# Frequency sets mirrored in PSUM, half-piece sums by accumulating DMAs and the fourth up-product last in a fixed order

## Chip, cores and metric

One core of a Trainium2 chip runs the program. TensorE (PE) multiplies, ScalarE (ACT) empties PSUM and computes activations, VectorE (DVE) does elementwise work in SBUF, GpSimd (POOL) does a few small operations and issues the DMAs of its queue, and SyncE (SP) issues the other DMAs. The metric is the device time of one execution in microseconds (us), as the median of several runs.

## What is computed

Two branches of one input x = A_q (2048 rows, 640 columns, bf16) are mixed row by row:

```python
g = sigmoid((x * gate_w).sum(-1, keepdims=True))
# branch A: long convolution by FFT over 2048 rows (padded to 4096), one per column
kv = shift_conv(k, shift_k, 4 taps) * v
y = irfft(rfft(kv, 4096) * rfft(ssm_k, 4096))[:2048]
a = x * (y + kv * ssm_D)
# branch B: a mixer and an MLP
h = gelu(layernorm(x) @ w1)            # 640 -> 640
x1 = x + shift_groups(h) @ w2
b = x1 + gelu(layernorm(x1) @ w3) @ w4 # 640 -> 1536 -> 640
out = g * a + (1 - g) * b
```

## The kernel before

Rows are kept as 2 chunks (c) of 128 partitions by 8 (rho). Branch B goes over four groups sc of two rho: mm1 (L967), mm2 (L1075), the third product ("up-product", L1129, 240 matmuls of 512 columns), then the fourth ("down-product", L1147, 4 x 24 matmuls of 320 columns for each sc). Each down-product is seeded by ACT, which copies x1 to PSUM (L1057), and is emptied by ACT with the factor 1 - g.

Branch A works on two column halves of 320. For each half and each of the signals h (the filter) and k (the convolved input):

- `forward` (L1167) multiplies by cosine and sine tables on PE (L1178). Frequencies are in two sets, kap 0 and kap 1; set 1 mirrors set 0. In set 0 each of 4 residues r and 2 parts (real, imaginary) takes 4 matmuls. In set 1 the even r add 2 matmuls to what set 0 left in PSUM (table FM2), the odd r take 4 of their own (FM1). ACT empties each result (128x640) into a slot, tags Sh and Sk.
- `unit` (L1277) is DVE's part, one per half and set: a butterfly on the h slot, a window (two adds) and a butterfly on the k slot, the complex product, and the fold. Slots hold 16 rows of 320 elements; sums and differences run mostly on whole slots, 128x2560 and 128x1280. One sum of each product, 128x2560, is made by a DMA that adds into its target (`add_dma`, L700, issued by POOL).
- `inverse` (L1313) multiplies by the inverse tables on PE: 8 output residues rho of 8 matmuls for each half (L1366, and L1341 for the last four of the second half, column chunk by chunk). ACT scales by g into one of four buffers XN (tag gy), DVE multiplies by q (`fin`), the sum with branch B goes into X by an accumulating DMA (first half, L1392) or by DVE (second half), and SP stores the rows.

All instructions are nodes of a graph. `schedule` and `_forward` (L181, L200) pick the next node of all engines by a modelled start time, with the list RANK as the priority among equals, and also pick the PSUM bank pair (4 pairs) of each job. Each engine then runs its nodes in that order and waits on semaphores for the rest. Every DVE add, subtract or multiply is recorded at L663, every eviction at L694, the second layernorm's ACT operations at L680, the DVE halves at L1351 to L1356. In the order that results, the last things on PE are the last four inverse rows of the second half. They can be multiplied only after DVE has finished the second half's last unit.

Of the kernel before, what the change touches and what calls it, by code (L numbers as in the profile page):

```python
# [7 lines left out]
U16 = mybir.dt.uint16  # L8
# [4 lines left out]
PAIRS = 4  # L13
# [75 lines left out]
class Prog:  # L89
    LAT = {"pe": (0.0, 0.20), "act": (0.24, 0.16), "dve": (0.12, 0.12), "pool": (0.2, 0.2), "sp": (0.1, 0.1)}  # L90
    LOOK = 1.0

# [86 lines left out]
    PRIO = ()  # L179

    def schedule(self):  # L181
        for n in self.nodes:
            n.base = frozenset(n.deps)
        for j in self.jobs:
            own = set(j.nodes)
            j.ext = [d for v in j.nodes if not v.first for d in v.base if d not in own]
            if j.seeded:
                j.nodes[0].soft = [d for v in j.pes for d in v.base if d not in own]
        for n in self.nodes:
            for d in n.deps:  # L190
                d.users.append(n)
        for n in self.nodes:
            n.prio = self.PRIO[n.idx]
        self._forward()

    RATE = 390e3
    WINDOW = 3.4133
    PHASE = 2.4

    def _forward(self):  # L200
        nodes = self.nodes
        for n in nodes:
            n.deps = set(n.base)
            n.missing = len(n.deps)
            n.start = n.end = None
        for j in self.jobs:
            j.pair = None
            j.left = len(j.evicts) if j.evicts else 1
        free = {"pe": 1.0, "act": 0.7, "dve": 0.8, "pool": 1.1, "sp": 0.7}
        ready = {e: [] for e in ENGS}  # L210
        known_at = {}
        pair_free = [0.0] * PAIRS
        pair_job = [None] * PAIRS
        bits = [[False, False] for _ in range(PAIRS)]
        link = 0.0
        xlink = 0.0
        alink = 0.0
        slink = 0.0
        warm = False
        window = -1  # L220
        duty = carry = 0.0
        busy, lock = False, 0.0
        LAT = self.LAT

        def arrive(n):
            at = 0.0
            for d in n.deps:
                t = d.end + (LAT[d.eng][0 if d.eng == n.eng else 1] if d.kind == "c" else 0.05)
                if t > at:
                    at = t  # L230
            known_at[n] = at
            ready[n.eng].append(n)

        for n in nodes:
            if n.missing == 0:
                arrive(n)
        left = len(nodes)
        order = {e: [] for e in ENGS}
        allseq = []
        while left:  # L240
            best = None
            for e in ENGS:
                for n in ready[e]:
                    t = max(known_at[n], free[e])
                    if n.first:
                        j = n.job
                        tp = None
                        for i in range(PAIRS):
                            if pair_job[i] is not None and pair_job[i].left:
                                continue  # L250
                            if j.seeded and not (bits[i][0] and bits[i][1]):
                                continue
                            if tp is None or pair_free[i] < tp:
                                tp = pair_free[i]
                        if tp is None:
                            continue
                        t = max(t, tp)
                        ok = True
                        for d in j.ext:
                            if d.end is None:  # L260
                                ok = False
                                break
                            if not n.seed:
                                t = max(t, d.end - n.cost)
                        if ok and n.seed:
                            for d in n.soft:
                                if d.end is None:
                                    ok = False
                                    break
                                t = max(t, d.end - self.LOOK)  # L270
                        if not ok:
                            continue
                    key = (t, -n.prio, n.idx)
                    if best is None or key < best[0]:
                        best = (key, n)
            assert best is not None, "schedule is stuck"
            n = best[1]
            e = n.eng
            t = best[0][0]
            ready[e].remove(n)  # L280
            n.start = t
            cost = n.cost
            if n.array:
                w = int((t - self.PHASE) // self.WINDOW)
                while window < w:
                    warm = duty > (0.42 if warm else 0.75) * self.WINDOW
                    window += 1
                    duty, carry = carry, 0.0
                if not warm:
                    cost += n.array  # L290
                if n.tag != "shk":
                    inside = min(cost, self.PHASE + (w + 1) * self.WINDOW - t)
                    duty += inside
                    carry += cost - inside
            if n.kind == "c" and e == "pool":
                if busy and free["dve"] > t + 0.2:
                    cost *= 2.2
                lock = t + cost
            elif e == "dve":
                busy = n.cost > 0.3 and n.tag[:2] != "bn"  # L300
                if busy and lock > t + 0.1:
                    cost += 0.48
                    lock = 0.0
            free[e] = t + cost
            if n.kind == "xpose":
                free[e] = max(free[e], link - 1.5)
            if n.kind == "c":
                n.end = t + cost
            elif n.kind == "dma":
                link = max(link, xlink, t + 1.2) + n.bytes / self.RATE  # L310
                n.end = link + n.land
            elif n.kind == "acc":
                alink = link = max(alink, link, t + 1.2) + n.bytes / 220e3
                n.end = alink + 1.6
            elif n.kind == "side":
                slink = max(slink, t + 1.0) + 0.2
                n.end = slink + (6.5 if link > t else 2.8)
            else:
                xlink = max(xlink, t + 1.3, link) + n.bytes / 190e3
                n.end = xlink + 0.5  # L320
            j = n.job
            if n.first:
                pick = None
                for i in range(PAIRS):
                    if pair_job[i] is not None and pair_job[i].left:
                        continue
                    if j.seeded and not (bits[i][0] and bits[i][1]):
                        continue
                    if pick is None or pair_free[i] < pair_free[pick]:
                        pick = i  # L330
                j.pair = pick
                if pair_job[pick] is not None:
                    old = pair_job[pick]
                    n.deps.update(old.evicts if old.evicts else old.pes)
                pair_job[pick] = j
                for b in range(2):
                    if j.bits[b] is not None:
                        bits[pick][b] = j.bits[b]
            if j is not None and (n in j.evicts or not j.evicts):
                j.left -= 1  # L340
                if j.left == 0:
                    ends = [v.end for v in (j.evicts or j.pes)]
                    pair_free[j.pair] = max(ends) + 0.1
            n.seq = len(allseq)
            n.ordinal = len(order[e])
            order[e].append(n)
            allseq.append(n)
            left -= 1
            for u in n.users:
                u.missing -= 1  # L350
                if u.missing == 0:
                    arrive(u)
        self.order = order
        self.allseq = allseq
        self.span = max(n.end for n in nodes if n.tag[:4] != "fill")
        while order["pe"][-1].tag[:4] == "fill":
            order["pe"].pop()
# [37 lines left out]
    def emit(self, block):  # L395
# [11 lines left out]
        for n in self.nodes:  # L407
            if n.kind != "c":
                n.sem = nc.alloc_semaphore(f"d{n.idx}")
# [104 lines left out]

def _tables():

# [929 lines left out]
```

## Time and profile before

| | |
|---|---|
| three runs | 225.49, 225.89, 226.24 us, median 225.89 us |
| profiled execution | span 223.5 us, 3945 instructions; 2.4 us less than the median of the runs lies between first and last instruction |
| PE clock granted | 0.998 over the span |
| DMA moved | 34.04 MB, of which 9.50 MB through POOL's queue |
| PE's last matmuls | from 215.83 us for 3.97 us |

The profiled execution has no time of its own outside its span; the 2.4 us between span and median is taken as what lies around every execution. "Busy" counts an instruction from start to end, and neighbours on one engine overlap a little, so a group's busy time divided by its count is what one more of its kind costs; the mean duration beside it is longer.

### The profile page before, as it was taken

What the parts mean: (1) busy time and instruction counts of PE and PEld (TensorE: products, weight loads), DVE (VectorE), ACT (ScalarE), POOL (GpSimd) and SP (SyncE); (2) the same over time, 40 slices, a digit from 0 to 9 for tenths busy, and PEclk for the clock granted to TensorE, in tenths of its full rate; (3) what the DMA queues carried; (4) which work ended last, traced back from release to release, by engine and by line L of the source; (5) the groups of instructions that cost most, each with busy time, mean ns of one, the idle gap of its engine ahead of it and who ended that gap; (6) DMA issues with size and microseconds to landing.
All of it is one profiled execution on the core that took longest, in us unless ns stands there. A gap on an engine that the chain in (4) does not pass through costs nothing.

```text
span 223.5 us, 3945 instructions
## 1 busy us (share of the span) xinstructions
PE 216.3 (97%) x1557; PEld 138.0 (62%) x1569; DVE 208.7 (93%) x267; ACT 174.6 (78%) x292; POOL 41.1 (18%) x48
## 2 busy tenths in 40 slices
PE   7999999999999999999999999999999999999993
PEld 7589655557676655457744455667745675577772
DVE  4999899999999899999899999799998999999976
ACT  3989999899999999999987488997145723572484
POOL 1335662403003120450200200000020002033020
PEclk9999999999999999999999999999999999999999
DMA  6999996589801968061654150003559000648667
GB/s 208 385 403 387 350 361 236 116 156 283 349 5 33 345 120 337 4 117 41 126 101 90 24 97 0 1 3 98 137 87 257 11 0 3 117 87 117 151 117 235
DMA packets 36713, 34.04 MB, mean 152 GB/s; under 512 B 17508, under 2 KB 31719, under 8 KB 36568
## 3 DMA queue, kind: packets, MB, share of 16 engines
q1 hardware_dynamic: 31560, 23.97, 35.8%
q0 software_dynamic: 4848, 9.50, 18.9%
q10 hardware_dynamic: 288, 0.33, 0.6%
q8 instruction: 12, 0.20, 0.4%
q14 instruction: 5, 0.04, 0.1%
HBM read 21.47 MB, written 3.93 MB: 114 GB/s over the span
## 4 chain that ended last, share of the span: by engine, by line
PE 76%; ACT 18%; DVE 2%; DMA 2%; issue 1%; SPq 0%; ACTq 0%
PE PS L1147 23%; PE PS L1129 23%; ACT arena L694 12%; PE PS L1178 9%; PE PS L967 8%; PE PS L1366 6%; ACT PS L1057 5%; PE PS L927 2%; ACT arena L680 2%; DVE arena L663 2%; DMA arena<-in_A_q_dram 2%; PE PS L823 1%; PE PS L769 1%; PE PS L758 1%; PE PS L780 0%
## 5 line engine op out<-in xcount | busy, mean ns | idle before, releaser
L663 DVE TENSOR_TENSOR arena<-arena 128x2560 bf16<-128x2560 bf16 (+5 forms) x175 | 186.1, 1116 | 7.0 <-ACT arena L694 3.5
L694 ACT ACTIVATE arena<-PS 128x640 bf16<-128x640 f32 (+8 forms) x142 | 104.2, 812 | 18.9 <-PE PS L1129 14.7
L1147 PE MATMUL PS<-arena 128*128 128x320 bf16 x384 | 53.3, 299 | 0.0
L1129 PE MATMUL PS<-arena 128*128 128x512 bf16 x232 | 52.2, 379 | 0.8 <-ACT arena L694 0.5
L1147 PEld LDWEIGHTS PS<-arena 128*128 128x128 bf16 x384 | 37.4, 98 | 15.0 <-issue 0.3
L694 ACT ACTIVATE arena<-PS,arena 128x320 bf16<-128x320 f32 (+1 forms) x47 | 27.7, 626 | 24.2 <-PE PS L1147 22.2
L1129 PEld LDWEIGHTS PS<-arena 128*128 128x128 bf16 x240 | 23.3, 98 | 27.4 <-issue 0.5
L1178 PE MATMUL PS<-arena 128*128 128x320 bf16 x224 | 34.4, 300 | 0.7 <-DVE arena L906 0.6
L1178 PEld LDWEIGHTS PS<-arena 128*128 128x128 bf16 x224 | 20.8, 98 | 12.8 <-ACT arena L694 2.8
L680 ACT ACTIVATE arena<-arena 128x640 bf16<-128x640 bf16 (+2 forms) x34 | 25.8, 787 | 0.8 <-DMA arena<-in_A_q_dram 0.4
L967 PE MATMUL PS<-arena 128*128 128x512 bf16 (+1 forms) x121 | 22.9, 335 | 0.2
L1075 PE MATMUL PS<-arena 128*128 128x320 bf16 x160 | 22.6, 299 | 0.0
L1057 ACT ACTIVATE PS<-arena 128x640 f32<-128x640 bf16 x32 | 22.3, 719 | 0.2
L868 POOL TENSOR_TENSOR arena<-arena 128x4 f32<-128x4 f32 (+1 forms) x9 | 14.0, 1553 | 30.7 <-DVE arena L668 30.4
L1075 PEld LDWEIGHTS PS<-arena 128*128 128x128 bf16 x160 | 15.4, 98 | 6.7 <-ACT PS L1057 0.6
L967 PEld LDWEIGHTS PS<-arena 128*128 128x128 bf16 x125 | 11.8, 98 | 8.2 <-ACT arena L694 0.5
L702 POOL DMA_DIRECT2D arena<-arena x4 | 4.8, 1202 | 57.6 <-DVE arena L663 57.6
L888 DVE BATCH_NORM_STATS2 arena<-arena 128x6 f32<-128x320 bf16 x28 | 12.4, 477 | 2.9 <-DMA arena<-in_A_q_dram 2.8
L1366 PE MATMUL PS<-arena 128*128 128x320 bf16 x96 | 14.3, 299 | 0.0
L1007 POOL DMA_DIRECT2D arena<-arena x18 | 9.7, 545 | 12.7 <-ACT arena L694 12.7
L1366 PEld LDWEIGHTS PS<-arena 128*128 128x128 bf16 x96 | 9.2, 98 | 4.3 <-issue 0.3
L1392 POOL DMA_DIRECT2D arena<-arena x4 | 5.1, 1276 | 35.7 <-ACT arena L694 25.9
(42 smaller groups left out, 81.5 us busy)
## 6 DMA issues: line engine op xcount, KB each, us to landing
arena<-in_B_w_dram POOLq DMA_DIRECT2D x4, 960.0 KB, 8.2
arena<-in_A_k_dram SPq DMA_DIRECT2D x4, 640.0 KB, 14.3
arena<-in_A_v_dram SPq DMA_DIRECT2D x4, 640.0 KB, 14.1
arena<-arena POOLq DMA_DIRECT2D x4, 640.0 KB, 6.1
arena<-in_A_q_dram SPq DMA_DIRECT2D x4, 640.0 KB, 7.4
out_dram<-arena SPq DMA_DIRECT2D x15, 160.0 KB, 2.0
arena<-in_A_q_dram SPq DMA_DIRECT2D x6, 320.0 KB, 5.5
arena<-in_A_ssm_k_dram SPq DMA_DIRECT2D x3, 512.0 KB, 11.5
```

The source lines that it names most:

```text
L663: return dve(lambda e: e.tensor_tensor(o, a, b, op), [a, b], [o], c_tt(n), tag=tag, **kw)
L680: node = P.op("act", lambda e, ps: e.activation(o, i, func, **kw), r=r, w=[o], cost=c_act(n, naps, acc is not None, psum=False), tag=tag, ...
L694: node = P.op("act", lambda e, ps: e.activation(ov, inner(ps), func, **kw), r=r, w=[o], cost=c_act(n, len(r), acc is not None), job=job, t ...
L868: P.op("pool", lambda e, ps: e.tensor_tensor(r, v, hv, ALU.pow), r=[v, HALF], w=[r], cost=cost, tag="ln")
L888: dve(lambda e, o=o, x=x: e.bn_stats(o, x), [x], [o], 0.393, tag="bn", group=("bn", id(mv), rho, c))
L967: fns.append(lambda e, ps, b=b, c=c, lhsT=lhsT: e.matmul(bank(ps, b, 256 * n), lhsT, XT[:, c, r0:r0 + n, :], start=(c == 0), stop=(c == 4)))
L1057: P.seed(job, lambda e, ps: e.activation(two(ps, 320), x, ACTF.Copy), [X[:, c, rho, :]], c_act(640, psum=False), tag)
L1075: fns.append(lambda e, ps, hh=hh, ft=ft, lhsT=lhsT: e.matmul(bank(ps, hh, 320), lhsT, w2v[:, ft, 320 * hh:320 * hh + 320], start=False, st ...
L1129: fns.append(lambda e, ps, b=b, ft=ft, c=c, sc=sc: e.matmul(bank(ps, b, 512), w3h[ft // 6][:, c, 128 * (ft % 6):128 * (ft % 6) + 128], XT[ ...
L1147: fns.append(lambda e, ps, hh=hh, ft=ft, lhsT=lhsT: e.matmul(bank(ps, hh, 320), lhsT, w4h[ft // 6][:, ft % 6, 320 * hh:320 * hh + 320], st ...
L1178: fns.append(lambda e, ps, w=w, b=b, rhs=rhs, st=(first and n == 0), en=(n == len(ss) - 1): e.matmul(bank(ps, b, 320), w, rhs, start=st, s ...
L1366: fns.append(lambda e, ps, w=w, z=z, c=c, st=(n == 0), en=(n == len(terms) - 1): e.matmul(bank(ps, c, 320), w, z[:, c, :], start=st, stop=en))
```

## The change

1. **Forward, set 1.** All four residues, for both signals and halves, are now made from the PSUM of set 0 by 2 matmuls. FM2 grows to 4 residues. Evictions get constant factors (2.0, root 2).
2. **Inverse, even rows.** DVE first makes, for the even residues, difference and sum of the two sets (tags mir0, mir1; the sum, mira, by DMA in the first half, by DVE in the second). Each even rho then takes 4 matmuls instead of 8.
3. **Units on half slots.** Differences are made by DVE, and sums by DMAs that add in place: both butterfly sums (128x2560), two sums of each product (tags pwTa, pwTb, pwSa, pwSb, 128x1280 in runs of 640 bytes), one more for three of the four units (pwTy, pwSy), and both fold sums. The product runs as two products T and S of half size. In set 1 the butterfly does the turn by root 2 itself, in pieces of 640 and 1280. In all there are 44 accumulating DMAs where there were 8.
4. **Order of the tail.** The four down-products of sc 3 are split into column halves and come last in the source. The output of both inverse halves is multiplied by q in place; for the residues of sc 3 the sum with branch B is made when the down-product is emptied: by ACT and a DVE add (first column half), by one DVE operation from PSUM (second).
5. **Fixed lists.** `_forward` is gone. RANK has 993 values and is the order itself; a list PAIR names the PSUM pair of each of 238 jobs. DMA semaphores of SP and ACT are shared.

Sorted by RANK, the list gives these orders, read with the order in which the code creates its nodes. PE: all of the first half's forward, then six up-products of sc 0 with the second half's forward between them and the four down-products; the rest of the second half's forward beside sc 1; first-half inverse rows between sc 2 and sc 3; two of the four last down-products; the whole second-half inverse; the other two down-products. DVE: each unit's steps interleaved so that other steps stand between a sum's issue and its use. POOL: the adds in the order of DVE's work, with the w4 load ahead of the first product's adds and the GM load ahead of the second unit's fold. ACT: the evictions of the second half's h set 1 begin among sc 0's last activations. They go into slot s3, which the first unit's S product uses as its temporary.

```diff
-    def _forward(self):
...
+    def schedule(self, rank, pairs):
+            n.prio = rank[n.idx]
+        self.allseq = sorted(self.nodes, key=lambda n: -n.prio)
+        self.order = {e: [n for n in self.allseq if n.eng == e] for e in ENGS}
...
+EVEN = (0, 1)
+BY_DMA = {("bh", 0, 0), ("bh", 0, 1), ("bk", 0, 0), ("bk", 0, 1), ("bh", 1, 0), ("bh", 1, 1), ("bk", 1, 0), ("bk", 1, 1),
+          ("pwa", 0, 0), ("pwa", 0, 1), ("pwa", 1, 0), ("pwa", 1, 1), ("fin", 0)}
+BY_DMA = BY_DMA | {("fold", 0, 0), ("fold", 0, 1), ("fold", 1, 0), ("fold", 1, 1), ("mir", 0), ("pwb",0,0),("pwb",0,1),("pwb",1,0),("pwb",1,1),("pwz",0,0),("pwz",0,1),("pwz",1,0)}
...
+        parts = ((0, 1),) if sc < 3 else ((0,), (1,))
...
-                if r % 2 == 0:
-                    go(job, lambda s: FM2[:, r // 2, ri, :], r, ri, (MIRROR[r // 2][ri],),
-                       S1_[:, r, ri if r == 0 else 1 - ri], False, sig)
+                if r % 2 == 0 or (sig, half) in R4M:
+                    go(job, lambda s: FM2[:, r, ri, :], r, (MIRROR[r // 2][ri],), S1_[:, r, ri if r < 2 else 1 - ri],
+                       ROOT2 if r % 2 == 0 else None, False, sig)
...
+        return P.dma("pool", lambda e, ps: e.dma_start(o, i, accum_op=ALU.add, max_dma_last_dim=2560), r=[o, i], w=[o], nbytes=256 * n,
+                     cost=1.15, kind="acc", tag=tag)
...
+        tt(D, lo, hi, ALU.subtract, 2560, tag=tag + "d")
+        add(lo, hi, 2560, dma, tag + "a")
...
+        tt(rb[0], kb[0], hb(1, 1), ALU.mult, 1280, tag=tag)
+        tt(tb[1], kb[1], hb(1, 0), ALU.mult, 1280, tag=tag)
+        add(fl(T, 1), fl(R, 0), 1280, da, tag + "a")
+        tt(rb[1], kb[0], hb(0, 1), ALU.mult, 1280, tag=tag)
+        tt(kb[1], kb[1], hb(0, 0), ALU.mult, 1280, tag=tag)
+        add(fl(K, 1), fl(R, 1), 1280, db, tag + "b")
+        tt(tb[0], kb[0], hb(1, 0), ALU.mult, 1280, tag=tag)
+        tt(kb[0], kb[0], hb(0, 0), ALU.mult, 1280, tag=tag)
+        tt(k[:, :, 0], k[:, :, 0], t[:, :, 1], ALU.subtract, 1280, tag=tag + "z")
+        add(k[:, :, 1], t[:, :, 0], 1280, dz, tag + "y")
...
+        add(S[:, 0:4], S[:, 4:8], 1280, dma, tag + "a")
+        add(T[:, 0:4], T[:, 4:8], 1280, dma, tag + "a")
...
+            tt(t4[:, a], x, y, ALU.subtract, 1280, tag=f"mir{a}")
+            add(x, y, 1280, ("mir", half) in BY_DMA, f"mira{a}")
```

More of the change, by code (lines that the diff above doesn't have):

```diff
@@ L189, in schedule @@
         for n in self.nodes:
             for d in n.deps:
[L191 to L198, printed above, removed]
-    def _forward(self):
[L201 to L357, printed above, removed]
@@ L1363, in inverse @@
+                z = odd if r % 2 else (x4, y4)
+                terms = [(GM[:, kap, ri, r, s, :], z[kap][:, r // 2, ri]) for kap in range(2) for ri in range(2)]
             fns, rd = [], [x for term in terms for x in term]
@@ L1402, in inverse, with bydma, units @@
         P.stage = ""
+    def bydma(what, half, kap):
+        return (what, half, kap) in BY_DMA
+    Y = [[], []]
+    parts = {}
+    def units(half, plan):
+        for step in plan:
+            what, kap = step[0], step[1]
+            P.stage = 2 * half + kap
+            if what in ("bh", "bk"):
+                if what == "bk":
+                    window(step[2], kap)
+                parts[what] = butterfly(step[2], step[3], step[4], kap == 1 and (what[1], half) in R4M,
+                                        bydma(what, half, kap), what)
+                if what == "bk":
+                    parts["y"] = parts["bk"]
+            elif what == "pw":
+                for i in range(2):
+                    product(parts["bh"][i], parts["bk"][i], step[2 + 2 * i], step[3 + 2 * i], bydma("pwa", half, kap),
+                            bydma("pwb", half, kap), bydma("pwz", half, kap), "pw" + "TS"[i])
+            else:
+                Y[half].append(fold(*parts["y"], step[2], step[3], bydma("fold", half, kap), "fold"))
+        P.stage = ""
@@ L1419, in bass_gated_mix__ssm_conv_h3__mixer_s_mlp__prompt_kernel @@
+    P.stage = 3
+    for i in range(4):
+        mm4(3, i)
+    P.stage = ""
+    P.schedule(RANK, PAIR)
     P.assign_waits()
```

432 lines of the change are left out of this document (203 added, 229 removed), and 94 rows, old and new, of tables (PAIR, RANK).

## Prediction

> **What bounds it now.** I read the busy shares first, then the chain that ended last, then stages.
>
> ```profile
> PE 216.3 (97%) x1557; PEld 138.0 (62%) x1569; DVE 208.7 (93%) x267; ACT 174.6 (78%) x292; POOL 41.1 (18%) x48
> ...
> PE 76%; ACT 18%; DVE 2%; DMA 2%; issue 1%; SPq 0%; ACTq 0%
> ```
>
> The first line has busy time by engine, the second the chain by engine. PE and DVE are both nearly full, so neither alone tells what an edit is worth. The chain in order of time (start, length, what) tells more:
>
> ```profile
> 72.45 9.74 ACT arena L694 x18
> 82.19 0.35 issue
> 82.54 4.26 PE PS L1129 x19
> ...
> 109.35 3.26 PE PS L1147 x24
> ...
> 214.91 1.10 PE PS L1366 x8
> 216.01 0.02 issue
> 216.03 0.95 ACT arena L694 x2
> 216.99 0.02 issue
> 217.01 3.98 DVE arena L663 x15
> ```
>
> Up to 82.5 us evictions on ACT are in the chain, then PE alone until 216, then the last residues' DVE work. The stage from 82.3 us to PE's last matmul, by window and by group (busy us, mean ns, idle before):
>
> ```profile
> 82.30:219.80 137.50, 136.86 (x856) 83.50 (x864) 131.69 (x146) 98.16 (x156) 16.72 (x13) 1.00 0.42 91
> ```
>
> ```profile
> L1178 PE MATMUL PS<-arena 128*128 128x320 bf16 x112 | 17.6, 300 | 0.0
> L1366 PE MATMUL PS<-arena 128*128 128x320 bf16 x96 | 14.3, 299 | 0.0
> L1341 PE MATMUL PS<-arena 128*128 128x320 bf16 x32 | 4.7, 299 | 0.0
> ```
>
> PE works 136.86 of 137.5 us, DVE 131.69. What PE loses there shortens the kernel, if DVE, only 5 us behind, comes along.
>
> **PE's part.** Set 1 from PSUM saves 4 odd jobs of 2 matmuls for each signal and half: 8 x 4 = 32. Mirrored rows save 4 x 4 for each half: 32. The first half's 16 forward matmuls lie before 82 us, where ACT is in the chain: counted at nothing, as ACT's evictions, still 64 of 128x640, cover them. That leaves the 112 - 96 = 16 forward matmuls of L1178 and 32 inverse ones, 48. One costs 3.26 / 24 = 0.136 us (the 109.35 row), not its mean of 300 ns, as matmuls overlap: **48 x 0.136 = 6.5 us**. Fills and split jobs stay under 1 us and are left in the range.
>
> **The tail.** The last matmuls, the operation that the new tail ends with, and a store of that size:
>
> ```profile
> 215.83 3.97 PE L1341 MATMUL PS<-arena 128*128 128x320 bf16 x28
> ```
>
> ```profile
> L1351 DVE SCALAR_TENSOR_TENSOR arena<-PS,arena x1: 544/544/544, 215.2 to 215.2; 128x320 bf16<-128x320 f32 x1
> ```
>
> ```profile
> L1356 SPq DMA_DIRECT2D out_dram<-arena x2: 344/408/472, 217.5 to 221.4; - x2
> ...
> DMA to landing us min/median/max: 1.6/1.7/1.7
> ```
>
> Now 223.5 - 219.8 = 3.7 us lie behind PE's end. After: one operation from PSUM 0.54, handoffs 0.3, store 1.7, about 2.6. SP has some 17 stores in that stretch at 0.41 each, 7 us of issue over 8 us of PE work, and 2.6 MB at the 303 GB/s that the end of the trace shows take 8.7 us:
>
> ```profile
> 219.00:222.00 3.00, 0.80 (x6) 0.35 (x4) 2.31 (x10) 1.35 (x3) 0.00 (x0) 1.00 0.98 303
> ```
>
> If they start late the tail grows by 1 to 2 us; I take 0 and keep 2 in the range. **With no new waits** PE ends at 219.8 - 6.5 = 213.3, the span at 215.9.
>
> **DVE's part.** Its groups (count, busy us, mean ns):
>
> ```profile
> L663 DVE TENSOR_TENSOR arena<-arena 128x2560 bf16<-128x2560 bf16 x74 | 108.0, 1493 | 3.6 <-ACT arena L694 1.6 <-DMA arena<-arena 1.0
> L663 DVE TENSOR_TENSOR arena<-arena 128x1280 bf16<-128x1280 bf16 x64 | 49.1, 821 | 0.5 <-ACT arena L694 0.2
> L663 DVE TENSOR_TENSOR arena<-arena 128x320 bf16<-128x320 bf16 x15 | 3.9, 320 | 0.0
> L663 DVE TENSOR_TENSOR arena<-arena 128x640 bf16<-128x640 bf16 x8 | 3.8, 489 | 1.4 <-ACT arena L694 1.4
> ...
> L668 DVE TENSOR_SCALAR arena<-arena 128x4 f32<-128x4 f32 x8 | 1.3, 164 | 0.0
> ```
>
> Busy over count gives 1.46, 0.767, 0.26 and 0.475 us. After the change there are 24, 132, 4 and 30 of them, and 4 operations from PSUM at 0.54: 35.0 + 101.2 + 1.0 + 14.3 + 2.2 = 153.7, against 165.3 with today's one PSUM operation. DVE gains 11.6 us, because two half pieces cost more than one whole (1.53 against 1.46). The 128x5120 ones stay.
>
> **The accumulating DMAs** go from 8 to 44. Their rows: POOL issues of L702 (640 KB) and L1392 (320 KB in runs of 640 bytes), and what DMA did behind them (window, then PE, PEld, DVE, ACT, POOL busy, clock, DMA share, GB/s):
>
> ```profile
> L702 POOL DMA_DIRECT2D arena<-arena x4: 1177/1196/1238, 94.5 to 196.9; - x4
> ...
>   DVE arena L663: 1.0, 3
> ...
> DMA to landing us min/median/max: 5.6/6.1/7.0
> ```
>
> ```profile
> L1392 POOL DMA_DIRECT2D arena<-arena x4: 1264/1277/1287, 188.4 to 212.5; - x4
> ...
> DMA to landing us min/median/max: 4.5/4.5/6.3
> ```
>
> ```profile
> 127.70:131.30 3.60, 3.60 (x28) 2.26 (x26) 3.56 (x3) 3.54 (x6) 0.00 (x0) 1.00 1.01 182
> 190.20:192.50 2.30, 2.30 (x13) 1.00 (x12) 2.27 (x3) 1.17 (x2) 0.00 (x0) 1.00 1.17 142
> ```
>
> So an add costs 1.2 us on POOL, starts 0.45 later, holds all 16 engines for **3.6 us** (640 KB) or **2.3 us** (320 KB in short runs), and releases its reader 0.45 after. 320 KB in longer runs isn't in the trace: between 1.8 (half of 3.6) and 2.3; I take 1.8. New queue time: 8 butterfly sums 28.8; 16 product sums and 3 pieces' worth of fin 19 x 2.3 = 43.7; 6 pwy, 8 fold, 2 mirror sums 16 x 1.8 = 28.8; together **101 us** (109 with 2.3), nearly all between 80 and 204 us, on one queue that holds 4 x 3.6 + 4 x 2.3 = 23.6 today. POOL issues 44 x 1.2 = 53 us.
>
> By the Trainium skill, "DMA: Bandwidth & Descriptors", section on the anatomy of one DMA, a DMA of this path takes 2.0 us plus its bytes at 436 GB/s, an estimate of 3.5 and 2.75 us here. The trace shows 6.1 and 4.5, so the measurement decides; by the page's figure the sum would be the fast rival's.
>
> **Walking DVE's list.** The page's GB/s in 40 slices prices the w4 load, which shares the adds' queue (960 KB at about 360, as in the better slices with loads, is 2.7 us):
>
> ```profile
> GB/s 208 385 403 387 350 361 236 116 156 283 349 5 33 345 120 337 4 117 41 126 101 90 24 97 0 1 3 98 137 87 257 11 0 3 117 87 117 151 117 235
> ```
>
> DVE can begin the first half's k difference at about 79 us: its inputs are among the evictions of the 72.45 row, and the list puts four fewer ACT operations ahead of the first layernorm sums. From there to the second half's first mirrored sum it has 124 x 0.767 + 7 x 1.46 + 16 x 0.475 + 11 small ones at 0.16 = 114.7 us. Add by add, one behind the other on the queue, the first unit goes so: the k sum is issued at 80.6 and holds the queue from 82.2 to 85.8; the w4 load stands behind it to 88.5; pwTa, pwTb, pwSa, pwSb follow at 2.3 each to 97.7; the S difference, which DVE reaches at 96.8, starts at 98.2: a wait of 1.4. POOL, in order, holds the next unit's h sum behind pwSy, which waits for the same. Further down: 0.75 at the fold, 2.1 (S difference), 0.3, 0.6 and 1.05 (fold) in the second unit, 1.85 in the third, 0.7 and 1.1 in the fourth, **9.8 us** in all. DVE gets there at 79 + 114.7 + 9.8 = 203.5.
>
> PE gets to the second half's inverse 13.0 us before its end (48 inverse and 48 down-product matmuls at 0.136): at 213.3 - 13.0 = 200.3. It waits for the mirrored sum until 203.7: **3.4 us**. The wait that goes is DVE's fin work behind the last inverse; what is late next is that sum. Two waits before it fall into the same 3.4: ACT's eviction into s3 waits for pwSb (98.2, ACT is there at about 95), and with it queue the evictions and seeds that PE needs; and the second half's first evictions into s0 for the second unit's T sums. They delay PE's arrival, not its release.
>
> **Sum:** 213.3 + 3.4 + 2.6 = 219.3 span, **+2.4 = 221.7 us**, 4.2 below the median.
>
> **Rivals.**
> - **Waits hidden.** Adds overlap more than one by one, or DVE starts earlier; the 3.4 goes: 215.9 + 2.4 = 218.3, and 215.6 if the first layernorm's 2.7 us reach PE as well. For it: three waits for an add today cost 1.0 us in all. Against: those adds stood alone.
> - **The queue becomes the bound (slower).** Place: POOL's queue from the first product on. Price: each 10% on an add's queue time moves the walk's end by 6 us (waits 9.8 to 16). It decides from 7% on, where the 4.2 are gone. At 10% the time is 227.7, at 15% 231. For it: 101 us of 124 are booked, and other transfers share the engines. The add issued at 163.36 ran into the q loads from 165.0 on, and its DVE reader started 6.7 us after the issue against 5.6 for the one at 196.94:
>
> ```profile
> 163.36 1.18 POOL L702 DMA_DIRECT2D arena<-arena  x1 [36.05 <-DVE arena L663]
> ...
> 196.94 1.18 POOL L702 DMA_DIRECT2D arena<-arena  x1 [7.27 <-DVE arena L663]
> ```
>
> ```profile
> 170.02 32.30 DVE L663 TENSOR_TENSOR arena<-arena 128x2560 bf16<-128x2560 bf16 x31 [0.62 <-DMA arena<-arena]
> 202.56 9.62 DVE L663 TENSOR_TENSOR arena<-arena 128x2560 bf16<-128x2560 bf16 x9 [0.24 <-DMA arena<-arena]
> ```
>
> The same page of the Trainium skill, section on queues, rings and completion order, has each DMA engine take turns between queues packet by packet; the trace agrees with these 6.7 us.
> - **Nothing arrives.** PE saves its matmuls but waits for sums by the same amount: 225.2 to 226.6.
>
> **Chances.** Forecast 0.36, hidden 0.24, queue 0.33, nothing 0.07. A measurement tells about 0.3% from no change; faster by more is 0.36 + 0.24 = 0.60, same 0.07, slower 0.33. The range runs from the hidden rival with the earlier start, less 1 us for the small terms left out, 214.5, to the queue at 18%, 233; it leaves out some 2 in 10.
>
> **What would show it.** Right: L1178 with 192 matmuls and inverse rows with 96; PE idle about 3 us before the second half's inverse; DVE waits for DMA near 10 us, most at the product's S difference and the folds; adds of 2.3 us on the queue; 2.6 us behind PE's end. Wrong: PE waiting for sums from the first unit on (the queue rival), DVE waits under 3 us (the hidden one), DVE's half pieces dearer than 0.767, or the first up-product away from 82.5.

## The result and the profile after

The changed kernel takes 255.48 us (median of four runs, 252.84 to 256.97) against 225.84 for the kernel before in the same comparison. The ratio is 1.122, with a 95% interval of 1.119 to 1.126. This ratio and those below are made from the faster runs of each kernel alone, here from 252.84 and 254.14 (granted clock 0.950 and 0.935 over the span), while the profile below is of the run of 256.97 (0.924). The forecast was 221.7 and faster, its range ended at 233. The profiled execution has a span of 255.2 us.

The page of the changed kernel, busy time by engine and the shares of the chain that ended last:

```profile
PE 222.6 (87%) x1499; PEld 136.4 (53%) x1512; DVE 197.0 (77%) x299; ACT 173.1 (68%) x293; POOL 86.3 (34%) x84
...
q0 software_dynamic: 17840, 22.29, 53.7%
q1 hardware_dynamic: 31176, 24.10, 34.8%
...
DVE 34%; DMA 34%; PE 12%; issue 12%; POOL 4%; ACT 2%; SPq 0%; DVEq 0%; POOLq 0%; ACTq 0%
```

DVE's 197.0 us are what was forecast (208.7 less 11.6). But no compute engine is as full as before, and a third of the chain is DMA, where PE alone had 76% in the kernel before. Queue q0, which carries POOL's DMAs (packets, MB, time as a share of 16 engines), holds 53.7% of 255.2 = 137 us of all 16 engines; q1, which carries SP's, holds 34.8%, 89 us.

The same stretch, 75 to 216 us, in the kernel before and then in the changed kernel, which has a longer one beside it (window; PE, PEld, DVE, ACT, POOL busy; clock; DMA share; GB/s):

```profile
75.00:216.00 141.00, 140.06 (x896) 85.40 (x902) 135.36 (x143) 101.77 (x161) 17.27 (x13) 1.00 0.43 93
```

```profile
75.00:240.00 165.00, 138.33 (x793) 78.91 (x801) 119.39 (x176) 98.82 (x157) 57.53 (x49) 0.91 0.97 155
75.00:216.00 141.00, 118.24 (x680) 67.03 (x688) 103.50 (x155) 87.78 (x137) 48.94 (x42) 0.92 0.97 155
143.00:161.00 18.00, 6.06 (x20) 2.33 (x20) 8.47 (x12) 3.42 (x5) 6.11 (x6) 0.64 0.94 159
```

The DMA share goes from 0.43 to 0.97: for 165 us the DMA engines are as good as full, 0.97 x 165 = 160 us of their time, in a kernel that had 141 us for the stage. (The share adds up the times of packets. They overlap a little, as the 1.17 of a row in the prediction shows, so 1 is no sharp limit.) What waits for them, from the changed kernel's waits (us in total, times, longest):

```profile
DVE arena L541 <- DMA arena<-arena: 30.7, 11, 9.8
...
PE PS L1044 <- DMA arena<-arena: 14.7, 2, 11.9
...
DVE arena L541 <- issue: 11.2, 4, 4.9
```

DVE waits 30.7 us for sums, and 11.2 us more in four waits for which this view names no releaser. Those are sums too: in the trace one of the adds lands 0.08 us before the end of each (at 104.51, 141.93, 159.99 and 225.49 us). PE waits 14.7 us for the layernorm transposes, in two pieces. These are the DMAs themselves, the adds first and then the transposes (issue in ns, minimum, median and maximum; who waited; us from issue to landing):

```profile
L1094 POOL DMA_DIRECT2D arena<-arena x44: 840/1264/2430, 75.7 to 233.0; - x44
...
DMA to landing us min/median/max: 3.6/6.4/10.8
```

```profile
L980 SPq DMA_TRANSPOSE arena<-arena x16: 1202/2325/3533, 76.3 to 177.5; - x16
...
  PE PS L1044: 14.7, 2
...
DMA to landing us min/median/max: 2.7/6.5/12.1
```

In the kernel before, the 16 transposes were issued in 1.27 us each, all between 74.6 and 119.7, and landed after 2.7:

```profile
L1102 SPq DMA_TRANSPOSE arena<-arena x16: 1199/1270/1284, 74.6 to 119.7; - x16
...
DMA to landing us min/median/max: 2.6/2.7/4.5
```

One place shows how it goes. First PE and then DVE of the changed kernel in order of time (start, length, operation, idle before and its releaser), then a part of its chain:

```profile
143.64 0.71 PE L1073 MATMUL PS<-arena 128*128 128x320 bf16 x4
156.29 11.26 PE L1044 MATMUL PS<-arena 128*128 128x512 bf16 x39 [11.94 <-DMA arena<-arena]
```

```profile
143.61 0.83 DVE L541 TENSOR_TENSOR arena<-arena 128x1280 bf16<-128x1280 bf16 x1 [0.78 <-ACT arena L572]
152.88 2.29 DVE L541 TENSOR_TENSOR arena<-arena 128x1280 bf16<-128x1280 bf16 x3 [8.44 <-DMA arena<-arena]
```

```profile
105.03 4.14 DMA arena<-arena
...
142.98 9.78 DMA arena<-arena
...
182.90 10.11 DMA arena<-arena
```

At 142.98 POOL issues the last sum of the second unit's product (pwSy) and 0.7 us later the 1 MB GM load; the transposes of the third row group are under way as well. The sum takes 9.8 us, where the same sum of the first unit, issued at 105.03, takes 4.1. DVE stands for 8.4 us, and PE stands for 11.9 us because a transpose is late. In 143 to 161 us PE works 6.06 of 18 us, and its granted clock falls to 0.64. At 182.90 it is the same for the third unit's sum, beside the q loads that SP issues from 180.87.

### The profile page after: what moved, and what is told of

It reads as the page before. It is cut to its first block, busy times and chain, and to the rows that moved or that the text cites. A ratio compares the mean times of both kernels' runs of the same rounds, so it can differ in the third digit from the quotient of the medians.

```text
span 255.2 us, 3918 instructions
## 1 busy us (share of the span) xinstructions
PE 222.6 (87%) x1499; PEld 136.4 (53%) x1512; DVE 197.0 (77%) x299; ACT 173.1 (68%) x293; POOL 86.3 (34%) x84
## 3 DMA queue, kind: packets, MB, share of 16 engines
q0 software_dynamic: 17840, 22.29, 53.7%
q1 hardware_dynamic: 31176, 24.10, 34.8%
## 4 chain that ended last, share of the span: by engine, by line
DVE 34%; DMA 34%; PE 12%; issue 12%; POOL 4%; ACT 2%; SPq 0%; DVEq 0%; POOLq 0%; ACTq 0%
DMA arena<-arena 32%; DVE arena L541 32%; PE PS L1015 5%; POOL arena L1094 3%; PE PS L845 2%; PE PS L1209 2%; POOL arena L746 1%; DMA arena<-in_A_q_dram 1%; ACT arena L572 1%; DVE arena L546 1%; PE PS L805 1%; PE PS L647 1%; PE PS L636 1%; ACT arena L558 1%; PE PS L701 0%
## 5 line engine op out<-in xcount | busy, mean ns | idle before, releaser
L541 DVE TENSOR_TENSOR arena<-arena 128x1280 bf16<-128x1280 bf16 (+6 forms) x204 | 173.7, 904 | 47.8 <-DMA arena<-arena 30.7
L572 ACT ACTIVATE arena<-PS 128x640 bf16<-128x640 f32 (+6 forms) x142 | 104.4, 814 | 30.9 <-PE PS L1044 23.8
L1094 POOL DMA_DIRECT2D arena<-arena x44 | 51.7, 1311 | 100.2 <-DVE arena L541 91.0
L1044 PE MATMUL PS<-arena 128*128 128x512 bf16 x231 | 59.3, 413 | 17.9 <-DMA arena<-arena 14.7
L1015 PE MATMUL PS<-arena 128*128 128x320 bf16 x384 | 57.0, 309 | 3.7 <-ACT arena L572 3.4
L572 ACT ACTIVATE arena<-PS,arena 128x320 bf16<-128x320 f32 (+1 forms) x48 | 25.7, 593 | 36.9 <-PE PS L1209 18.0
L1044 PEld LDWEIGHTS PS<-arena 128*128 128x128 bf16 x240 | 24.7, 105 | 48.7 <-issue 26.2
L1015 PEld LDWEIGHTS PS<-arena 128*128 128x128 bf16 x384 | 38.5, 101 | 21.0 <-ACT arena L572 3.7
L1073 PE MATMUL PS<-arena 128*128 128x320 bf16 x192 | 32.3, 304 | 4.3 <-ACT arena L572 3.8
L1073 PEld LDWEIGHTS PS<-arena 128*128 128x128 bf16 x192 | 17.2, 99 | 15.1 <-ACT arena L572 7.4
L845 PE MATMUL PS<-arena 128*128 128x512 bf16 (+1 forms) x121 | 24.3, 353 | 0.2
L953 PE MATMUL PS<-arena 128*128 128x320 bf16 x160 | 22.7, 299 | 0.0
L953 PEld LDWEIGHTS PS<-arena 128*128 128x128 bf16 x160 | 15.3, 98 | 6.5 <-issue 0.4
L845 PEld LDWEIGHTS PS<-arena 128*128 128x128 bf16 x125 | 12.4, 103 | 9.2 <-issue 0.5
L1209 PE MATMUL PS<-arena 128*128 128x320 bf16 x96 | 14.7, 304 | 0.2 <-DVE arena L541 0.2
L636 PE MATMUL PS<-arena 128*128 128x128 bf16 x85 | 11.9, 260 | 2.5 <-DVE arena L594 1.4
L546 DVE TENSOR_SCALAR arena<-arena 128x640 bf16<-128x640 bf16 (+3 forms) x31 | 10.7, 360 | 3.2 <-PE PS L805 2.1
L885 POOL DMA_DIRECT2D arena<-arena x18 | 9.8, 553 | 7.9 <-ACT arena L572 7.9
```

Of the source, the lines that this page charges most:

```text
L541: return dve(lambda e: e.tensor_tensor(o, a, b, op), [a, b], [o], c_tt(n), tag=tag, **kw)
L572: node = P.op("act", lambda e, ps: e.activation(ov, inner(ps), func, **kw), r=r, w=[o], cost=c_act(n, len(r), acc is not None), job=job, t ...
L845: fns.append(lambda e, ps, b=b, c=c, lhsT=lhsT: e.matmul(bank(ps, b, 256 * n), lhsT, XT[:, c, r0:r0 + n, :], start=(c == 0), stop=(c == 4)))
L953: fns.append(lambda e, ps, hh=hh, ft=ft, lhsT=lhsT: e.matmul(bank(ps, hh, 320), lhsT, w2v[:, ft, 320 * hh:320 * hh + 320], start=False, st ...
L1015: fns.append(lambda e, ps, hh=hh, ft=ft, lhsT=lhsT: e.matmul(bank(ps, hh, 320), lhsT, w4h[ft // 6][:, ft % 6, 320 * hh:320 * hh + 320], st ...
L1044: fns.append(lambda e, ps, b=b, ft=ft, c=c, sc=sc: e.matmul(bank(ps, b, 512), w3h[ft // 6][:, c, 128 * (ft % 6):128 * (ft % 6) + 128], XT[ ...
```

## Experiments

**Theory A:** the 16 DMA engines are overbooked. Adds, transposes and loads hold each other up, and the time is the engines' time. **Theory B:** each add costs a fixed time, by its latency and POOL's issue in order, and the fixed list was laid out for other latencies. **Theory C:** only the adds' own queue counts. **Theory D:** DVE's amount of work sets the time. "Engine time of the adds" below is q0's share times the span, less the 12.1% x 221.1 = 26.8 us of the first run. That run's thin adds are in the 26.8: the kernel before, without its 8 adds, has 18.9% x 223.5 - 23.6 = 18.6 us on q0, and with that the adds' time comes out 8 us higher in every run.

**Thin adds.** Every add moves one run of 16 elements per partition; the rest of each sum is left out.

```diff
-e.dma_start(o, i, accum_op=ALU.add, max_dma_last_dim=2560)
+cut = (slice(None),) + (slice(0, 1),) * (len(o.shape) - 2) + (slice(0, 16),)
+e.dma_start(o[cut], i[cut], accum_op=ALU.add)
```

> All 44 accumulating DMAs keep their place, issue, waits and semaphores, but each moves one run of 16 elements per partition instead of its whole piece, so the sums are left out. Theory A (the 16 DMA engines are overbooked: adds, transposes and loads lengthen each other): the waits of DVE and PE for DMAs nearly vanish, DVE's fall from 31 us to under 8 and PE's from 15 to under 2, and the time falls to 216-224 us. Rival B (each add's fixed time, POOL's issue of 1.2 us in order, and a list planned for other latencies): the waits stay, 240 us or more.

Measured: 224.61 us (222.31 to 225.84), ratio 0.992 (0.987 to 0.996), 0.6 us above theory A's range. Its busy times, queues, the stage from 75 to 216 us, and its waits:

```profile
PE 210.7 (95%) x1512; PEld 131.5 (59%) x1512; DVE 196.2 (89%) x299; ACT 172.8 (78%) x293; POOL 74.0 (33%) x84
...
q1 hardware_dynamic: 31176, 24.10, 39.4%
q0 software_dynamic: 7984, 5.75, 12.1%
```

```profile
75.00:216.00 141.00, 137.00 (x864) 81.81 (x864) 125.34 (x191) 104.33 (x171) 44.85 (x49) 1.00 0.37 71
```

```profile
DVE arena L541 <- ACT arena L572: 12.1, 8, 4.4
...
DVE arena L541 <- DMA arena<-arena: 1.5, 2, 0.9
```

The same 44 issues, waits and order are 31 us faster when they move hardly any bytes. So what is lost goes with what the adds move, and theory B's fixed part is no more than what is left. (POOL's issues are shorter here, 0.85 us in the median against 1.26; the next run, with 1.18, shows that this isn't the loss.) The rest of the change is worth 0.8% even so. And the transfers that aren't adds hold 0.37 x 141 = 52 us of engine time in the stage: with the adds' 110 that makes 162 us for 141. The packets of q1 take 39.4% x 221.1 = 87 us here and 89 beside the full adds. So the transfers of SP don't take longer on the engines beside adds; they wait longer for them.

**Half the bytes.** Each add moves half of its elements, and half of every sum is left out.

```diff
+cut = (slice(None), slice(0, o.shape[1] // 2)) if len(o.shape) < 4 else (slice(None), slice(0, 1))
-e.dma_start(o, i, accum_op=ALU.add, max_dma_last_dim=2560)
+e.dma_start(o[cut], i[cut], accum_op=ALU.add, max_dma_last_dim=2560)
```

> The changed kernel as it is, list and issues and waits too, but each of the 44 adds moves only half of its elements (half of every sum is left out): 8.4 MB in place of 16.7. With all bytes it takes 255.5 us, with hardly any 224.6. Theory A (the 16 engines are full from 75 us on): time is lost only where the booked engine time passes what the stage has; half the adds' 120 us is 60, which with the 40 us of the other transfers fits into the stage, so much more than half of the 30.9 us goes: 227 to 234 us. A straight line in the bytes (each add's own length on the path, no queueing) gives the middle, 240 us. Theory B (the number of adds) would leave it above 250, which the thin run already speaks against.

Measured: 228.41 us (225.88 to 231.93), ratio 1.003 (0.999 to 1.008). Its queue and its stage:

```profile
q0 software_dynamic: 10672, 13.93, 34.0%
```

```profile
75.00:216.00 141.00, 133.97 (x842) 79.59 (x848) 124.78 (x188) 104.31 (x173) 53.67 (x50) 1.00 0.71 128
```

Engine time of the adds is 34.0% x 227.0 - 26.8 = 50 us, and 52 + 50 = 102 of 141 is 0.72, where the row has 0.71. From hardly any bytes to half the time rises by 4 us (the ratio from 0.992 to 1.003), from half to all by 27 (1.003 to 1.122). A price for each byte from the first one on would give a straight line, so the bend speaks for a resource that fills up. It doesn't prove it: adds that are hidden until DVE's list has no slack left would give a bend too. The time falls by 27 us with every issue in its place, so the number of issues and the list alone aren't what is wrong with the full adds.

**Copies for adds.** The same DMAs overwrite their target where they added to it, so the sums are left out (`accum_op=ALU.add` removed).

> The changed kernel as it is, but the 44 DMAs copy their source over their target where they added it (the sums are left out): same bytes from source to target, same runs of elements, issues, waits and order. If the engine time of an add comes from the adding (it reads the target as well), a copy holds the engines for about half as long, q0 falls from 137 to some 80 us of engine time, and the time is near that of the run with half the bytes: 226 to 232 us. If it comes from the bytes and the runs of 640 bytes, a copy costs the same, and it stays at 250 to 256.

Measured: 228.88 us (226.37 to 232.62), against 226.10 for the kernel before in the same comparison.

```profile
q0 software_dynamic: 5968, 22.29, 30.4%
```

All bytes still move, 22.29 MB on q0, but in 5968 packets instead of 17840, and the engine time goes from 110 us to 30.4% x 225.5 - 26.8 = 42. So it is the adding that fills the engines: an add holds them 2.6 times as long as a copy of the same bytes (118 and 50 us, 2.4 times, with the 18.6 from above). The adding changes two things at once. The source is added into the target, and the packets are small: in the trace's records an add has 640, 1280 or 2560 bytes in a packet, a copy mostly 4480 or 5120. So the expectation's "same runs of elements" doesn't hold for the packets, and which of the two weighs more stays open.

**Thin transposes.** The 16 layernorm transposes move one of their five blocks; four fifths of the transposed rows are left out.

```diff
-e.dma_start_transpose(o, b)
+e.dma_start_transpose(o[:, 0:1, :], b[:, 0:128])
```

> The 16 layernorm transposes by DMA move one block of 128 columns instead of five, so four fifths of that transposition is left out; everything else as in the change. Theory A: the transposes are both victims and part of the load; PE's 14.7 us of waits for them shrink to under 4, the adds land somewhat sooner, and the time falls by 10 to 18 us to 237-245. Rival C (the adds' own queue is alone the bound, PE's waits for transposes lie beside DVE's and cost nothing): 250-256, as DVE's waits stay.

Measured: 245.98 us (245.48 to 246.49), ratio 1.089 (1.082 to 1.096), 1 us above theory A's range. Its stage, and who waited for DMAs:

```profile
75.00:216.00 141.00, 124.90 (x747) 71.20 (x745) 108.06 (x161) 93.76 (x146) 51.70 (x43) 0.98 0.91 152
```

```profile
DVE arena L541 <- DMA arena<-arena: 23.3, 9, 8.2
...
PE PS L1044 <- DMA arena<-arena: 2.0, 2, 1.1
```

DVE's wait for sums falls from 30.7 to 23.3 us, PE's for transposes from 14.7 to 2.0, and the stage's share from 0.97 to 0.91. The transposes take part in the crowding with 9.5 us (7.5 by the ratios), the adds carry most of it. **Both thin** leaves hardly any bytes after the loads:

> The adds move one run of 16 elements for each partition and the transposes one of five 128-column blocks (the sums and four fifths of the transposed layernorm rows are left out); issues, waits and order stay. It shows what of the time stays when hardly any bytes are moved after the loads. Theory A: near the run with thin adds alone, 221 to 225 us, because transposes are short once the adds do not share the engines; so the list, VectorE and TensorE alone allow about that. Theory B (latencies and issue order): the same or up to 3 us less. Under 218 us would say that the transposes alone, without the adds, also set the time.

Measured: 224.28 us (221.43 to 225.70), ratio 0.990 (0.986 to 0.994), no better than thin adds alone. Without the adds the transposes cost nothing that shows.

**Fewer adds, the changed kernel's own list.** Three sets of sums go back to DVE, each at the place where its add was issued: the 8 butterfly sums (36 adds stay), all but first product sums and `fina` (12 stay), and all but butterflies, first product sums and `fina` (20 stay).

```diff
+BY_DMA = {x for x in BY_DMA if x[0] not in ("bh", "bk")}              # 36 stay
+BY_DMA = {x for x in BY_DMA if x[0] in ("pwa", "fin")}                # 12 stay
+BY_DMA = {x for x in BY_DMA if x[0] in ("bh", "bk", "pwa", "fin")}    # 20 stay
```

> The eight butterfly sums (128x2560) are made by DVE again, at 8 x 1.46 = 11.7 us; all other adds stay DMAs. Theory A: 29 us of queue time go, waits of DVE fall by more than 11.7, the time falls to 232-243. Rival B: fewer round trips help as well, 235-245. Rival D (DVE's amount of work is what counts): the time rises by up to 12 us, 255-267.

> Only the sums pwTa and pwSa and the first half's fin sums stay DMAs, 12 instead of 44; the other 32 are made by DVE, 8 x 1.46 + 24 x 0.767 = 30 us more on it (227 us in all). Theory A: DVE becomes the bound without waits, 232-240 us. Rival D: 255 or more. In both the matmuls saved are worth nothing as long as DVE is full.

> The 20 adds of the run with a new list (butterflies, first product sums, last sums), but in the changed kernel's own order, with the 24 other sums on VectorE at the places where they were issued. Theory A: the booked engine time is the same as with the new list (about 78 us on q0, loads included), so most of the 21 us is saved here too: 234 to 241 us. If the list is what saved them (theory B), it stays near the 250.7 that the new list alone reached with 44 adds, or above: 246 to 254.

Measured (median of all runs; the ratio is to the kernel before), with the same list, and below it with new lists that were laid out with the adds' measured rates:

| adds, list | engine time of adds | DVE busy, us | time, us | ratio (95%) |
|---|---|---|---|---|
| 44, as changed | 110 | 197.0 | 255.48 | 1.122 (1.119 to 1.126) |
| 36, same list | 76 | 207.4 | 254.22 | 1.126 (1.106 to 1.145) |
| 20, same list | 51 | 213.4 | 237.79 | 1.047 (1.041 to 1.054) |
| 12, same list | 21 | 224.7 | 244.54 | 1.083 (1.064 to 1.102) |
| 44, new list | 107 | 198.8 | 250.66 | 1.100 (1.091 to 1.109) |
| 36, new list | 74 | 208.7 | 248.48 | 1.095 (1.090 to 1.100) |
| 20, new list | 53 | 212.3 | 234.54 | 1.039 (1.034 to 1.044) |

With 12 adds DVE is the fullest engine:

```profile
PE 219.8 (90%) x1512; PEld 136.1 (56%) x1512; DVE 224.7 (92%) x331; ACT 173.5 (71%) x293; POOL 56.4 (23%) x52
```

So DVE's amount of work counts at that end and the adds at the other, but neither range holds for 12 adds: theory A had 232 to 240, rival D 255 or more. For 20 adds theory A's 234 to 241 holds. 20 adds are still slower than the kernel before. One reason is that half pieces, turned butterflies and mirror sums give DVE more work, 213.4 us against 208.7; with 12 adds, which move about the bytes of the 8 before, it is 224.7. It isn't the only reason, as the last experiment below has 203.1 us and is no faster.

Theory A missed with the 36 adds. It said 232 to 243 and nothing came, though 34 us of engine time went (rival D's 255 to 267 begins 0.8 us above). Nor does the sum over the stage forecast it: 52 + 76 = 128 us would fit into 141. In stretches of 10 us the DMA share of this run goes from 0.30 (205 to 215 us) to 1.14 (175 to 185), and DVE's longest wait, 7.4 us, ends at 147.3 behind an add issued at 137.05, in stretches with 1.10 and 1.07. The engines are crowded in bursts, which a mean over the stage hides. That the bursts alone keep this run slow is not shown, as DVE has 10 us more work in it too. It matters which adds go: taking off the 24 that turn 44 into 20 (7.9 MB) gains 18 us, with DVE's added work counted in, taking off the 8 of the butterflies (5.2 MB) 1 us, which is inside the noise.

**New lists.** RANK is replaced, and for 36 and 20 adds BY_DMA is cut as above.

> The changed kernel with all its 44 adding DMAs, its operations and its sums as they are; only the fixed list of the order (the 993 ranks) is another one, worked out for adds of 125 to 170 KB per microsecond that share the 16 DMA engines with the transposes and the loads. Theory A (the engines' time is overbooked): no order of the same transfers helps much, because 120 us of engine time of the adds and some 40 us of the other transfers have to pass between 75 us and the last sum whatever their order: 245 to 256 us. Theory B (the list was laid out for other latencies, and another order hides them): 225 to 238 us.

> The 8 butterfly sums on VectorE, as in the run that gained nothing with the changed kernel's own list (254.2 us), and a list of the order worked out anew for these 36 adds (11.5 MB). If what kept that run slow was the list, laid out for other places of the sums, it falls to 234 to 242 us, between the 250.7 of 44 adds and the 234.5 of 20 adds with new lists. If it is the 36 adds of 320 KB themselves (theory A with a price by piece, not by byte: 36 x 2.3 = 83 us of engine time), it falls less, to 243 to 250.

> Only 20 of the 44 adds are left to the DMA engines (the 8 of the butterflies with 640 KB, the 8 first product sums and the 4 last ones, 8.8 of 16.7 MB); the others go back to VectorE, and the list of the order is worked out anew for that. Theory A: the adding queue needs about 65 us of engine time in place of 137, the waits on DMA go, and VectorE takes over 24 half pieces at 0.77 us (+18 us of busy time, about 215): the end is set by VectorE and TensorE together at 226 to 236 us. Theory B (each add costs by itself and by its issue on GpSimd): it falls by the share of adds removed, 24 of 44 of the 30 us, to 238 to 242 us. Either way not clearly under the kernel before.

The kernel with 44 adds and the new list:

```profile
75.00:240.00 165.00, 146.84 (x960) 87.00 (x968) 128.75 (x192) 110.59 (x183) 59.86 (x51) 0.99 0.97 163
```

Another order keeps PE's clock at 0.99, where it was 0.91, and gains 5 us; the DMA share stays at 0.97 and the time above 245. So the slow clock isn't what most of the time is lost by. With 20 adds the new list brings 3 us more than the old one; the adds that went are worth 18 us with the old list and 16 with the new ones. The 36 adds with a new list gain 6 us, much as the 44 did, and stay at 248.5, in the range of a price by piece. A list at fault would have given more by the expectation, though only one other list was tried. The stage and the wait of that run:

```profile
75.00:240.00 165.00, 145.84 (x929) 85.95 (x937) 138.66 (x197) 109.15 (x180) 52.66 (x43) 0.97 0.79 139
```

```profile
DVE arena L542 <- DMA arena<-arena: 15.3, 8, 4.6
```

The stage's share is 0.79 and DVE waits 15.3 us for sums: the engines aren't full on the mean of the stage, yet sums come late. Whether the small sums are dear because of the bursts, or because their readers come soon after them in DVE's list, was not tried by itself, and stays open.

**Parts 1 and 2 undone, 20 adds.** `R4M = set()` and `EVEN = ()`: the odd residues of set 1 take 4 matmuls again and the even inverse rows 8. RANK and PAIR are new lists for this graph.

> Parts 1 and 2 of the change undone: the odd residues of set 1 take their own 4 matmuls again, and the even inverse rows 8 (R4M and EVEN empty), so TensorE has 64 matmuls of 320 columns more, and VectorE loses the turned butterflies and the mirror operations (about 12 us). 20 adds by DMA as in the run with 20, and a list worked out for this graph. If VectorE is what bounds the run with 20 adds (212 of 232 us busy there), the 64 matmuls cost nothing that shows: 228 to 234 us, the same or less than that run's 234.5. If the saved matmuls are worth their 6.5 us, it is slower than that run: 238 to 242 us.

Measured: 238.41 us (235.05 to 239.43), ratio 1.043 (1.034 to 1.052); span 233.3 in the profile against 232.2 of the run with 20 adds and the mirrors. Busy times with the mirrors undone, and then with them:

```profile
PE 220.4 (94%) x1570; PEld 138.4 (59%) x1583; DVE 203.1 (87%) x299; ACT 174.8 (75%) x293; POOL 60.7 (26%) x60
```

```profile
PE 212.3 (91%) x1511; PEld 132.2 (57%) x1523; DVE 212.3 (91%) x323; ACT 174.9 (75%) x293; POOL 60.0 (26%) x60
```

The mirrors take 8.1 us from PE and give 9.2 to DVE. The median is at the edge of the second range, the span 1 us above the run with mirrors, and the intervals of the two ratios overlap: whether the mirrors gain a few us or nothing is not settled; they gain no more than that. DVE has 5.6 us less work here than the kernel before, so its work alone doesn't explain why this version is slower. No version found here is faster than the kernel before.

## Why the prediction was wrong

**What failed is the step "the accumulating DMAs"**, which the walk of DVE's list then built on. It booked 101 us on the adds' queue against the 124 us between 80 and 204, and walked "add by add, one behind the other on the queue". Its size was about right: the adds hold 110 to 118 us of engine time. Its resource was wrong. A queue with 19% left would be no bound, but the 16 engines under it also carry the transposes, the w4, GM and q loads and the stores. The share of 0.42 over 137.5 us stood in the row that the prediction quoted for PE's stage: 57.8 us of engine time, of which 23.6 were the old adds. The other 34 and the new 101 make 135 us in a stage of 137.5, before any lengthening. With the measured 52 and 110 it is 162 for 141. Half the bytes, which do fit, take 228; all of them don't and take 255. The thin, the half and the copying adds show that the loss goes with the adds' time on the engines and hardly with their issues or the list. They don't show that the sum over the stage alone decides: the 36 adds fit by that sum, 128 of 141, and took 254, with 10 us more of work on DVE. How much of the 44 adds' loss lies in bursts is open.

- **Waits.** Forecast for DVE 9.8 us; measured 30.7 + 11.2 = 41.9, which is 32.1 more. The span came out 255.2 against 219.3, 35.9 more. So most of it is DVE's waits behind the sums. The second half's inverse, which was to start at 203.7, starts at 237.1: 33.4 us are lost by then. PE's forecast wait of 3.4 us for the mirrored sum did not come: its inverse rows wait under 1 us for DVE in all, as PE itself was late by then.
- **Transposes.** They had no term. SP's queue was counted only at the stores. The transposes land after 6.5 us instead of 2.7 and cost PE 14.7 us of waiting; made thin, they give 7.5 to 9.5 us back.
- **The queue rival** had the direction, with 0.33, and named what lay behind it, that other transfers share the engines. Its price, 6 us for each 10%, was linear in an add's length, and 233 at 18% was as far as it went. The queue's own time is 9 to 17% above the 101 us (110 to 118), for which that price gives 227 to 232; the rest of the loss it lacks. The bend of the three byte amounts (224.6, 228.4, 255.5) is nothing that a linear price can give. Its sign of being right, PE waiting for sums, came in another form: PE waits for transposes.
- **The Trainium skill** was weighed at this step. "DMA: Bandwidth & Descriptors", section on queues, rings and completion order, has an engine take turns between its queues. The prediction let it speak for one late reader and did not go on to a sum over all queues. The transposes' row agrees with the taking of turns: 2.7 to 6.5 us.
- **With no new waits** the forecast was a span of 215.9. Thin adds come nearest to that, with 221.1: PE's busy time falls by 216.3 - 210.7 = 5.6 us, but its idle time grows from 7.2 to 10.4, and DVE waits 12.1 us for ACT's evictions. So with this list the hidden rival's time of 218.3 was out of reach too, as even thin adds take 224.6.
- **Off by little:** the first up-product comes at 85.6 us, forecast 82.5, and 3.8 us lie behind PE's end, forecast 2.6.
- **Right:** 192 forward and 96 inverse matmuls; 128x1280 at 101.1 us for 132, 0.766 each, and DVE at 197.0; issues of 1.2 us, 51.7 us in all.

```profile
L541 DVE TENSOR_TENSOR arena<-arena 128x1280 bf16<-128x1280 bf16 x132 | 101.1, 819 | 42.9 <-DMA arena<-arena 29.6 <-issue 11.2 <-ACT arena L572 1.6
```

```profile
L1094 POOL DMA_DIRECT2D arena<-arena x44 | 51.7, 1311 | 100.2 <-DVE arena L541 91.0
```

## What to carry to other kernels

Book DMAs by engine time, not by queue: take the DMA share of the stage in the profile before, times its length, add what the change adds, and compare with the stage. Here 162 us for 141 cost 31 us, 102 cost 4, and transfers that were not touched became late. A sum that doesn't fit is a warning; one that fits is no promise, as the 36 adds show (128 of 141, and nothing gained), so do it for short stretches as well. Work taken off DVE by an adding DMA is moved, not removed, and an add holds the engines more than twice as long as a copy.

## What the runs showed of the hardware

- An accumulating DMA held the 16 engines 2.4 to 2.6 times as long as a copy of the same bytes (110 and 42 us for 16.7 MB, or 118 and 50 by the other base) and split q0's transfers into 17840 packets instead of 5968. POOL's issue took 1.26 us in the median against 0.73. The Trainium skill, "DMA: Bandwidth & Descriptors", rules for kernel authors, says that an accumulate reads its destination and writes it later; a longer hold agrees with that, the factor isn't given there.
- With the engines full, issues took longer as well: a transpose occupied SP's queue for 2.33 us in the median, for 1.24 with thin adds and 1.27 in the kernel before. The time that q1's packets held the engines hardly changed, 89 us beside the full adds and 87 beside thin ones; what grew is the time to landing.
- PE's granted clock fell to 0.64 over the 18 us in which it stood for 11.9: the trace has 1.00 up to 147 us, 2.7 us after PE's last matmul, and 0.50 from 149 to 161, 4.7 us into its next ones. For the same matmuls PE was busy 222.6 us in the changed kernel and 210.7 with thin adds. By the Trainium skill, "TensorE: Matmul & The Clock Gate", part 1, an idle window of about 3.4 us brings half the clock; the trace agrees with its 0.50.
